# Lightning attention and a sin² feed-forward layer on one core: chunk 1's second projection by seven products of quarters, some forty copies free to run on another engine, and new order tables

## The chip, the core and the metric

One Trainium2 chip, one of its cores. The time is device microseconds from start to end of one execution. A core has a matmul engine (TensorE, PE in the profile, with its weight loads as PEld), VectorE (DVE), ScalarE (ACT), GpSimd (POOL) and SyncE (SP), each with its own list of instructions that it runs in order, and 16 DMA engines that move data between HBM and the on-chip memory. PE writes into eight accumulator banks of 128 x 512 f32 (PSUM).

## The reference, cut to what matters

```python
# attention: B, H, S, D = 4, 8, 768, 64; blocks along the sequence
intra = (q_blk @ k_blk.T * Dmask) @ v_blk          # Dmask[i, j] = lam**(i - j) for i >= j, else 0
inter = (q_blk * lam**(pos + 1)) @ kv_state
out   = intra + inter
kv_state = lam**block * kv_state + (k_blk * lam**(block - 1 - pos)).T @ v_blk
# feed-forward: x is out as [3072 tokens, 512], w_in [512, 2048], w_out [2048, 512]
h = x @ w_in
s = np.sin(alpha * h)
g = h + s * s / (alpha + 1e-09)
y = (g @ w_out).astype(np.float32)                 # the only output
```

## The kernel before

**Tiling.** The 3072 tokens are 24 blocks of 128 tokens for the attention and six chunks of 512 tokens (four blocks each) for the feed-forward layer. All matmuls take bf16 operands.

**Attention of a block.** q and k are scaled by powers of lam (`scale_block`, L454; the powers come from iotas on POOL and exponents on ACT at the start), transposed on PE (`piece_Q`, `piece_K`, `piece_T`; results copied to `qkT`), multiplied to scores in banks 1 and 2, which DVE multiplies by the mask into `Sm` (L623, "the mask product"), and multiplied with v (`part_O`, `piece_G`). Bank 7 holds the running state, which is copied to `Zc` or `Zd` (`part_Z`). The block's output is copied to `xT` (`part_O`'s `then`, `evict` L734). v is cast to bf16 on its way (`v2`). The first four blocks are made in smaller pieces ahead of everything else.

**First projection.** For each of 16 slices of 128 columns of w_in, `unit_A` (L807) runs four matmuls of 512 tokens into a bank; `unit_A2` (L845) does two slices for 256 tokens in eight matmuls. Here such a group of matmuls is called a unit. Behind each unit stand a sine on ACT (L832, L866), a square on ACT or POOL (L836/L837, L870/L871), and on DVE the sum h + s²/alpha into `gT` (L839, L874), which reads the unit's bank again and so sets it free. From chunk 1 on, the units share banks 4, 5 and 6.

**Second projection, two ways.** For chunks 0 and 1, `unit_B` (L880) runs 16 groups of four 512-wide matmuls (L887), and ACT copies each finished 128 x 512 result out (`osb`), from where ACT's queue stores it. For chunks 2 to 5 (`SC = 2`) the product of gT and w_out is split into quarters and made from seven products instead of eight: `weight_sums` (L914) forms five sums of quarters of w2 once (`Tw` in the ring `ws`, `Ta`, and two in place in `w2`; L930), `token_sums` (L933) forms for each quarter `p` of a chunk four sums of quarters of gT (two into `Xs`, two in place; L953) and, after product k = 1, four late ones in place (`late_sums`). `product` (L1037) runs one of the seven products for one half `u` of the rows: eight 256-wide matmuls (`unit_P`, L975), 14 such products in a chunk, in the order 3, 4, 2, 5, 1, 6, 7. `finish` (L1003) combines them: products 3 and 1 are copied (`kept`, on ACT), the others added or subtracted on DVE; SP stores the results. Each sum of quarters may run on POOL or DVE, as the tables say.

**Order.** Nothing is scheduled on the chip. `op` records every operation with what it reads and writes; `_Plan.ORDER` holds one list of operation numbers for each engine, written out by hand, and `_settle` goes through the lists; `emit` adds the semaphore waits, leaving out those that an earlier wait already covers. An operation whose engine is given as one name has to stand in that engine's list; one with several choices may stand in any of them. Pairs such as (42,112) in PE's list are fillers: so many matmuls of that many columns on unused data (`spin`, L1131), without a result.

**The main loop** (from L1136) runs the 16 units of chunk 0, the attention of blocks 4 to 11 between the groups of chunk 0's second projection and the units of chunk 1, and then for each chunk c from 2 to 5 its 16 units, the attention of the next blocks, the token sums of chunk c (for c >= SC) and the second projection of chunk c - 1. The weight sums stand ahead of the loops for chunks 2 and 3. After the loop come the 14 products of chunk 5. In chunk 2 (`c <= SC`) the attention's output takes bank 0 or 3, later one of banks 4 to 6 (`other()`).

**Other names that the change touches.** `QD` names which of the first four q scalings run on DVE. `cast_w1_first` (L381) casts the first half of w_in's first columns from `ws`, two 1024-column parts on DVE. The mask is made by POOL selects (`affine_select`), kept in a row by a common key `"select"`. `warm` is an exponent on ACT without use, ahead of the real ones.

## Time and profile before

Three runs took 210.68, 211.11 and 211.37 us, median 211.11. The profiled execution has a span of 209.8 us.

| | PE | DVE | ACT | POOL | DMA |
|---|---|---|---|---|---|
| busy, us | 203.5 | 160.3 | 158.7 | 126.9 | |
| share of the span | 97% | 76% | 76% | 60% | |
| instructions | 1975 | 266 | 294 | 130 | |
| 0 to 19 us | 16.00 | 12.61 | 13.02 | 10.59 | 99% |
| 193 to 209.8 us | 14.18 | 9.02 | 2.71 | 2.91 | 36% |

The granted clock of PE is 1.00 in all stages. The program moves 33.35 MB, of them 27.28 read from HBM. Of the chain that ended last, PE has 83%, DVE 6%, transfers 3% and SP's queue 3%; by line, the units of the first projection (L822, L856) hold 37%, the products (L975) 22%, the groups of the old second projection (L887) 13%.

How to read the rows that follow: a group's row has the line, the engine, the operation, the tiles written and read with their sizes, the count, then busy time in us, the mean of one in ns, and the engine's idle time just before them with what ended most of it. A row of the timeline or of the chain begins with the start in us and the duration. A row of windows has the stretch, its length and each engine's busy time with its number of instructions.

### The profile page before, as it was taken

The numbers are of one execution on the slowest core, as the hardware profiler recorded it, in microseconds if no ns is written. First come the engines' busy times: TensorE is split into PE (matmuls) and PEld (weight loads), VectorE is DVE, ScalarE is ACT, GpSimd is POOL, SyncE is SP. The second block draws the span as 40 slices with busy tenths as digits, with TensorE's granted clock in tenths as the row PEclk, the third lists the DMA queues.
The fourth block names the chain that finished last, engine by engine and source line by source line (L and its number), as shares of the span: only waits on it lengthen the run. The fifth ranks groups of instructions, "written<-read, shape, count | busy, mean of one in ns | idle before, by whom it ended". The sixth has DMA issues, their size and how long they took to land.

```text
span 209.8 us, 4867 instructions
## 1 busy us (share of the span) xinstructions
PE 203.5 (97%) x1975; PEld 134.3 (64%) x1975; DVE 160.3 (76%) x266; ACT 158.7 (76%) x294; POOL 126.9 (60%) x130
## 2 busy tenths in 40 slices
PE   7979999999999999999998999999999999999995
PEld 6847444457677776555555667766667765666894
DVE  4884557563999866868899799889698699777643
ACT  4949995968998989999997887787963889568210
POOL 7075354994469578679885392944581957378300
DMA  4999999999998999999999920190000004000514
GB/s 141 310 318 232 206 213 237 246 229 256 220 264 205 227 245 230 223 233 196 246 271 228 213 53 0 33 271 2 3 0 3 0 23 179 3 0 0 200 40 163
DMA packets 78998, 33.35 MB, mean 159 GB/s; under 512 B 55408, under 2 KB 76160, under 8 KB 78976
## 3 DMA queue, kind: packets, MB, share of 16 engines
q1 hardware_dynamic: 73744, 27.14, 56.2%
q0 software_dynamic: 3696, 3.67, 10.5%
q10 hardware_dynamic: 1536, 2.24, 3.3%
q8 instruction: 15, 0.25, 0.5%
q14 instruction: 7, 0.06, 0.1%
HBM read 27.28 MB, written 6.29 MB: 160 GB/s over the span
## 4 chain that ended last, share of the span: by engine, by line
PE 83%; DVE 6%; DMA 3%; SPq 3%; ACT 2%; issue 1%
PE bank L822 27%; PE bank L975 22%; PE bank L887 13%; PE bank L856 10%; DMA v<-in_v_dram 3%; PE bank L716 3%; SPq L315 3%; PE bank L612 3%; DVE gT L839 2%; PE bank L694 1%; DVE Sm L623 1%; PE bank L511 1%; PE bank L656 1%; DVE w L930 1%; PE bank L534 1%; PE bank L707 1%
## 5 line engine op out<-in xcount | busy, mean ns | idle before, releaser
L822 PE MATMUL bank<-xT,w 128*128 128x512 bf16 x296 | 70.5, 379 | 0.0
L839 DVE SCALAR_TENSOR_TENSOR gT<-u,rinv,bank 128x512 bf16<-128x512 bf16 x74 | 53.6, 742 | 18.2 <-ACT u L836 12.5
L832 ACT ACTIVATE t<-bank,alpha 128x512 bf16<-128x512 f32 x74 | 50.0, 684 | 21.0 <-PE bank L822 20.5
L822 PEld LDWEIGHTS bank<-xT,w 128*128 128x128 bf16 x296 | 28.3, 98 | 28.4 <-DVE gT L839 0.4
L836 ACT ACTIVATE u<-t 128x512 bf16<-128x512 bf16 x59 | 36.5, 628 | 1.3
L837 POOL TENSOR_TENSOR u<-t 128x512 bf16<-128x512 bf16 x15 | 16.0, 1066 | 34.1 <-ACT t L832 30.5
L953 POOL TENSOR_TENSOR gT<-gT 128x512 bf16<-128x512 bf16 x24 | 27.8, 1172 | 11.2 <-DVE Xs L953 6.0
L623 DVE TENSOR_TENSOR Sm<-bank,mask 128x1024 bf16<-128x1024 f32 x24 | 29.1, 1218 | 4.3 <-PE bank L648 1.8
L887 PE MATMUL bank<-w,gT 128*128 128x512 bf16 x128 | 31.4, 380 | 0.0
L874 DVE SCALAR_TENSOR_TENSOR gT<-u,rinv,bank 128x256 bf16<-128x256 bf16 x44 | 18.8, 476 | 7.8 <-ACT u L870 6.1
L472 POOL TENSOR_TENSOR qk<-q,Lq 128x512 bf16<-128x512 f32 x20 | 21.2, 1075 | 2.8 <-DMA q<-in_q_dram 2.8
L856 PE MATMUL bank<-xT,w 128*128 128x256 bf16 x176 | 22.2, 273 | 0.0
L492 POOL TENSOR_TENSOR qk<-k,Lk 128x512 bf16<-128x512 f32 x20 | 20.9, 1053 | 0.6 <-DMA k<-in_k_dram 0.6
L866 ACT ACTIVATE t<-bank,alpha 128x256 bf16<-128x256 f32 x44 | 18.9, 476 | 2.0 <-PE bank L856 1.5
L887 PEld LDWEIGHTS bank<-w,gT 128*128 128x128 bf16 x128 | 11.7, 98 | 12.2
L856 PEld LDWEIGHTS bank<-xT,w 128*128 128x128 bf16 x176 | 16.4, 98 | 3.5 <-issue 0.3
L953 POOL TENSOR_TENSOR Xs<-gT 128x512 bf16<-128x512 bf16 x13 | 16.1, 1235 | 1.5 <-DVE gT L839 1.4
L975 PE MATMUL bank<-w,gT 128*128 128x256 bf16 (+1 forms) x136 | 16.3, 266 | 0.0
L975 PE MATMUL bank<-w,Xs 128*128 128x256 bf16 (+1 forms) x136 | 16.0, 267 | 0.1
L975 PE MATMUL bank<-ws,gT 128*128 128x256 bf16 x128 | 15.8, 273 | 0.0
L975 PEld LDWEIGHTS bank<-w,gT 128*128 128x128 bf16 x136 | 12.6, 98 | 3.2
L975 PEld LDWEIGHTS bank<-w,Xs 128*128 128x128 bf16 x136 | 12.4, 98 | 2.8 <-DVE osb L1021 0.3
(101 smaller groups left out, 276.0 us busy)
## 6 DMA issues: line engine op xcount, KB each, us to landing
q<-in_q_dram SPq DMA_DIRECT2D x12, 512.0 KB, 6.2
k<-in_k_dram SPq DMA_DIRECT2D x24, 256.0 KB, 5.5
v<-in_v_dram SPq DMA_DIRECT2D x24, 256.0 KB, 5.4
out_dram<-osb SPq DMA_DIRECT2D x14, 256.0 KB, 2.5
w<-in_moe_w_out_dram POOLq DMA_DIRECT2D x4, 512.0 KB, 11.4
w<-in_moe_w_in_dram POOLq DMA_DIRECT2D x3, 512.0 KB, 9.0
ws<-in_moe_w_in_dram SPq DMA_DIRECT2D x2, 512.0 KB, 7.5
out_dram<-osb ACTq DMA_DIRECT2D x8, 128.0 KB, 4.0
```

The source lines that it names most:

```text
L472: lambda e, a=a: e.tensor_tensor(qk2[:, j:j + 2, 4 * a:4 * a + 4, :], q32[:, jq, 4 * a:4 * a + 4, :, :].rearrange("p h t d -> p t h d"), b ...
L492: lambda e: e.tensor_tensor(qk2[:, j, H:2 * H, :], block32(k32, jl), lk, ALU.mult), 1.05,
L623: op("DVE", lambda e: e.tensor_tensor(Sm[js][:, :, :], banks[:, 512 * b0:512 * b0 + 1024].rearrange("p (c i) -> p c i", i=128), bass.AP(ma ...
L822: ins = e.matmul(ps[hb][:, c0:c1], w1[:, kc, 128 * m:128 * (m + 1)], xT[x][:, kc, c0:c1], start=(kc == 0 and c0 == lo), stop=(kc == NKC - ...
L832: op("ACT", lambda e: e.activation(t16[ju][:, w], ps[hb][:, w], ACTF.Sin, scale=alpha[:, m:m + 1]), 0.69 if hi - lo == TCH else 0.475, [ba ...
L836: lambda e: (e.activation(u16[ju][:, w], t16[ju][:, w], ACTF.Square) if e is nc.scalar else e.tensor_tensor(u16[ju][:, w], t16[ju][:, w], ...
L839: op("DVE", lambda e: e.scalar_tensor_tensor(out=gT[g][:, m, w], in0=u16[ju][:, w], scalar=rinv[:, m:m + 1], in1=ps[hb][:, w], op0=ALU.mul ...
L856: ins = e.matmul(ps[hb][:, 256 * i:256 * i + 256], w1[:, kc, 128 * (m + i):128 * (m + i + 1)], xT[x][:, kc, lo:lo + 256], start=(kc == 0 a ...
L866: op("ACT", lambda e, i=i: e.activation(t16[ju][:, 256 * i:256 * i + 256], ps[hb][:, 256 * i:256 * i + 256], ACTF.Sin, scale=alpha[:, m + ...
L887: ins = e.matmul(ps[ob][:, w], gT[g][:, m, 128 * s4:128 * (s4 + 1)], w2[:, m, w], start=(m == 0), stop=(m == NM - 1),)
L953: e.tensor_tensor(dst, in0, in1, alu), 0, rd, wr))
L975: ins = e.matmul(ps[ob][:, lo + d0:lo + d1], lhs, rhs[:, d0:d1], start=first and p == 0, stop=(p == NM // 2 - 1), skip_group_check=True)
```

## The change

- `SC` goes from 2 to 1: chunk 1's second projection is made by the seven products too. Both sets of weight sums are recorded ahead of chunk 1's second half of units, chunk 1's token sums behind every second of these, and the second projection of chunk 1 by `product` (with chunk 2's attention outputs in one of banks 4 to 6).
- About forty copies and scalings that had a fixed engine, or one of two, may stand in the list of any of two or three: `AD` is ACT or DVE, `DP` DVE or POOL, `ADP` all three. They are the casts of w1, the first q scalings, the k scalings, the v casts, the copies of q and k transposes, of the state, of the attention outputs and of the second projection's results.
- POOL's selects lose their common key; instead `emit` makes a POOL operation that is marked `some`, and the one behind it, wait for the operation before it (`strict`). The exponents on ACT read `warm`, so that they stand behind it.
- All five order tables are new. The fillers, 102 in ten places of PE's list with 112 to 512 columns, become 22 of 512 columns at its head.

The core of the diff:

```diff
@@ class _Plan: ORDER @@
-            (42,112), 39, (30,128), 57, (11,128), 55, (1,128), 53, (1,128), 59, (8,128), 61, (1,512), 62,
-            (3,512), 65, 67, 69, 70, (3,512), 73, 75, 78, 80, 82, 85, (2,512), 87, 90, 91, 93, 124, 130, 140,
...
+            (22, 512), 39, 53, 59, 57, 55, 61, 62, 67, 69, 70, 65, 75, 78, 82, 73, 80, 87, 85, 90, 91, 93, 124,
+            130, 136, 140, 151, 147, 144, 159, 167, 163, 155, 175, 183, 171, 230, 228, 229, 191, 187, 206, 207,
...
@@ _ordered, emit @@
-        if d.eng != o.eng or d.dma is not None:
+        if d.eng != o.eng or d.dma is not None or d is o.strict:
...
+        last = None
+        for o in order:
+            if o.eng == "POOL" and o.dma is None:
+                if last is not None and (o.some or last.some):
+                    o.strict = last
+                    o.deps.add(last)
+                last = o
@@ sizes @@
-    SC = 2
-    QD = ((0, 0), (0, 2), (1, 0), (1, 2))
+    SC = 1
+    AD = (("ACT", 0, 0), ("DVE", 0, 0))
+    DP = (("DVE", 0, 0), ("POOL", 0, 0))
+    ADP = (("ACT", 0, 0), ("DVE", 0, 0), ("POOL", 0, 0))
@@ cast_w1_first @@
-                    op("DVE",
+                    op(AD,
@@ scale_block @@
-                            ported(op(QE(a, t),
+                            ported(op(DP,
...
-                        eng, dur = ("DVE", 0.68) if s + a < 3 else ("POOL", 1.05)
-                        ported(op(eng, lambda e, a=a: e.tensor_tensor(
+                        ported(op(DP, lambda e, a=a: e.tensor_tensor(
...
-                ported(op((("ACT", 0.62, 0.0), ("POOL", 1.05, 0.3)) if s > 11 else "ACT",
+                ported(op(ADP,
@@ part_Z, then @@
-                        op("ACT" if s < NP else (("ACT", 0.36, 0.0), ("DVE", 0.43, 0.0)), lambda e, r=r: (e.copy if e is nc.scalar else e.tensor_copy)(
+                        op(AD, lambda e, r=r: (e.copy if e is nc.scalar else e.tensor_copy)(
@@ unit_B @@
-                op("ACT", lambda e: e.copy(osb[jo][:, w], ps[ob][:, w]), 0.59, [bank(ob)], parts)
+                op(AD, lambda e: (e.copy if e is nc.scalar else e.tensor_copy)(osb[jo][:, w], ps[ob][:, w]), 0.59, [bank(ob)], parts)
@@ finish @@
-                    op("ACT", lambda e: e.copy(c1 if i == 1 else ny, got), 0.59 if n == 2 else 0.37, [bank(ob)], kc if i == 1 else kn)
+                    op(AD, lambda e: (e.copy if e is nc.scalar else e.tensor_copy)(c1 if i == 1 else ny, got), 0.59, [bank(ob)], kc if i == 1 else kn)
@@ main loop @@
             pieces = pieces_of(8, None, False) + pieces_of(10, 9, False)
+            if SC == 1:
+                weight_sums(True)
+                weight_sums(False)
             for i in range(8):
                 unit_A2(1, 2 * i, 1, (5, 6, 4)[(i + 2) % 3])
+                if SC == 1 and i % 2:
+                    token_sums(1, i // 2)
...
-                if c == SC + 1:
+                if c == SC + 1 and SC > 1:
                     weight_sums(False)
```

By the new tables, the first cast of w1 stands in ACT's list and the second in DVE's, chunk 1's sixteen token sums are ten on DVE and six on POOL, its four late ones two on each, chunk 5's four late sums are all on POOL, and the loads of w2 (issued from POOL's list) stand further behind in it.

More of the change, by code (lines that the diff above doesn't have):

```diff
@@ L31, in __init__ @@
         self.knows = None
+        self.some = False
+        self.strict = None
 class _Plan:
@@ L413, in _ @@
                 out=identf[:, :], in_=identf[:, :], pattern=[[-1, 128]], compare_op=ALU.not_equal,
[L414 removed]
+                fill=1.0, base=0, channel_multiplier=1), 0.5, ["identf"], ["identf"])
             op("DVE", lambda e: e.tensor_copy(ident[:, :], identf[:, :]), 0.2, ["identf"], ["ident"])
@@ L446, in _ @@
             op("ACT", lambda e: e.copy(alpha[:, :], ps[4][:, 0:NM]), 0.2, [bank(4), "warm"], ["alpha"])
-            def QE(s, a):
-                return "DVE" if (s, a) in QD else "POOL"
             def ported(o):
@@ L538, in piece_Q @@
                     if len(tbs) == 2:
-                        op("ACT", lambda e, a=a: e.copy(qkT[:, jt:jt + 2, 2 * a:2 * a + 2, :], tps[a]),
+                        op(AD, lambda e, a=a: (e.copy if e is nc.scalar else e.tensor_copy)(
+                            qkT[:, jt:jt + 2, 2 * a:2 * a + 2, :], tps[a]),
                            0.59, [bank(tbs[a])], [("qT", jt, a), ("qT", jt + 1, a)])
@@ L569, in piece_K @@
                 for t in range(2):
-                    op("ACT" if s else (("DVE", 0.43, 0.0), ("ACT", 0.6, 0.0)),
+                    op(AD,
                        lambda e, t=t: (e.copy if e is nc.scalar else e.tensor_copy)(qkT[:, jt + t, 4:8, :], tps[t]),
```

34 lines of the change are left out of this document (16 added, 18 removed), and 107 rows, old and new, of the table ORDER.

## The prediction, made before the changed kernel ran

> **What bounds the kernel now.** I read the page's first line, then the busy time by stage (cut where chunk 0 starts, where block 6 is scored, in chunk 2, where the loads end, where the last products begin), then the chain of waits.
>
> ```profile
> span 209.8 us, 4867 instructions
> ```
>
> ```profile
> 19.00:52.80 33.80, 33.80 (x243) 18.44 (x242) 19.42 (x30) 27.14 (x51) 19.58 (x17) 1.00 1.16 228
> 52.80:90.00 37.20, 37.20 (x432) 25.39 (x432) 31.27 (x58) 34.25 (x74) 26.56 (x27) 1.00 1.03 232
> 90.00:130.00 40.00, 39.33 (x345) 23.00 (x343) 35.45 (x52) 34.48 (x61) 28.41 (x25) 1.00 0.92 183
> 130.00:193.00 63.00, 63.00 (x517) 41.89 (x515) 52.56 (x83) 47.09 (x79) 38.83 (x35) 1.00 0.14 43
> ...
> sum 209.80, PE 203.51 PEld 134.30 DVE 160.35 ACT 158.69 POOL 126.87; mean PE 33.92 PEld 22.38 DVE 26.72 ACT 26.45 POOL 21.15
> ```
>
> The columns are the stretch, its length, then the busy time (and instructions) of PE, weight load, DVE, ACT and POOL, the granted clock and the DMA share. From 19 us to 193 the matmul engine has no hole but 0.67 us, in 90:130. So whatever leaves its list there is gained, unless another engine becomes the slower one. Next in line is the vector engine: 84% busy in 52.8:90 (31.27 of 37.20), 89% in 90:130.
>
> ```profile
> 7.63 6.83 DMA v<-in_v_dram
> ...
> 15.79 0.73 ACT xT L739
> ...
> 19.16 0.87 PE bank L856 x8
> ...
> 51.46 0.22 PE bank L511 x4
> ...
> 59.38 0.49 PE bank L534 x8
> ...
> 61.84 0.86 PE bank L887 x4
> ...
> 65.10 0.33 PE bank L612 x8
> 65.43 0.34 PE bank L707 x8
> 65.77 0.34 PE bank L716 x8
> 66.24 1.85 PE bank L856 x16
> ...
> 162.74 0.87 PE bank L975 x8
> ```
>
> The chain gives the start (a load of v that lands at 14.46, then ScalarE's copies in a row, then the first unit at 19.16) and the prices on the matmul engine: a group of the old second projection 0.86 (L887), a product of quarters 0.87 (L975), a unit of the first projection 0.87, one whole attention block 1.14 (65.10 to 66.24).
>
> **The change, part by part.**
>
> *Chunk 1's second projection.* 16 groups of four 512-wide matmuls go, 14 products of eight 256-wide ones come: 16 x 0.86 - 14 x 0.87 = 13.8 - 12.2, so **-1.6 us** on the engine that sets the end. No row leaves room for another size: both kinds ran back to back.
>
> *What it costs beside.* Chunk 1 now needs 16 token sums and four late ones, two copies and five additions for its results in place of four copies, and both sets of weight sums have to be ready two chunks' work earlier. The order tables put 12 of the 20 token sums on VectorE, 8 on GpSimd. The open engines also move work: by the tables v's casts go from ScalarE 20 and GpSimd 4 to ScalarE 5, GpSimd 10, VectorE 9; k's scalings on VectorE from 3 to 8; squares on GpSimd from 22 to 29. So ScalarE gets room that no part of the matmul engine waits for, and VectorE and GpSimd lose theirs. Prices:
>
> ```profile
> L839 DVE SCALAR_TENSOR_TENSOR gT<-u,rinv,bank 128x512 bf16<-128x512 bf16 x74 | 53.6, 742 | 18.2 <-ACT u L836 12.5 <-POOL u L837 5.2
> L623 DVE TENSOR_TENSOR Sm<-bank,mask 128x1024 bf16<-128x1024 f32 x24 | 29.1, 1218 | 4.3 <-PE bank L648 1.8 <-PE bank L612 1.5 <-PE bank L656 1.0
> L874 DVE SCALAR_TENSOR_TENSOR gT<-u,rinv,bank 128x256 bf16<-128x256 bf16 x44 | 18.8, 476 | 7.8 <-ACT u L870 6.1 <-POOL u L871 1.5
> L953 DVE TENSOR_TENSOR Xs<-gT 128x512 bf16<-128x512 bf16 x19 | 12.3, 658 | 0.1
> L953 DVE TENSOR_TENSOR gT<-gT 128x512 bf16<-128x512 bf16 x24 | 12.2, 532 | 0.1
> ...
> L726 DVE CAST xT<-bank 128x512 bf16<-128x512 f32 x7 | 5.1, 734 | 1.3 <-PE bank L716 1.1 <-PE bank L656 0.3
> ...
> L930 DVE TENSOR_TENSOR w<-w 128x1024 bf16<-128x1024 bf16 x3 | 3.3, 1105 | 0.0
> ...
> L930 DVE TENSOR_TENSOR ws<-w 128x1024 bf16<-128x1024 bf16 x2 | 1.4, 700 | 0.0
> L516 DVE COPY qkT<-bank 128x512 bf16<-128x512 bf16 x5 | 2.1, 424 | 2.3 <-PE bank L511 2.3
> ...
> L571 ACT COPY qkT<-bank 128x512 bf16<-128x512 bf16 x3 | 1.7, 588 | 1.6 <-PE bank L560 1.5
> L543 ACT COPY qkT<-bank 128x1024 bf16<-128x1024 bf16 x1 | 1.0, 1012 | 0.8 <-PE bank L534 0.8
> ...
> L953 POOL TENSOR_TENSOR gT<-gT 128x512 bf16<-128x512 bf16 x24 | 27.8, 1172 | 11.2 <-DVE Xs L953 6.0 <-DVE gT L953 5.0
> ```
>
> These are groups with their shapes kept apart: count, busy time, mean of one in ns, idle time before them. I counted the new tables where it is tightest, from the scores of block 6 to the first half of product 5 of chunk 1. VectorE's list there, from block 6's mask product to the token sum that this product reads, holds 73 instructions: 38 gT of 256 columns x 0.43 = 16.2; 2 gT of 512 x 0.72 = 1.4; 7 mask products x 1.21 = 8.5; 10 token sums x 0.57 (24.5 for 43) = 5.7; 3 weight sums in place x 1.10 and one other x 0.70 = 4.0; 12 copies and additions at 0.4 to 0.73 = 6.1. That is 41.9. Neighbours overlap in such sums (all of VectorE's groups add up to 170, its busy time to 160.35), so x 0.94: **39.5 us**. The matmul engine's list between the same two points: 31 units, groups and products x 0.865 = 26.9; seven attention blocks x 1.14 = 8.0; two pairs of q transposes x 0.49 and four of k x 0.22 = 1.9: **36.8 us**. VectorE works in order, a unit's bank isn't free before its gT is made, and there are three such banks; so the matmul engine can't run away, and if VectorE never idled the matmul engine would still lose 2.7 us. Both ends of this term: 0 if all sums run at their shortest (0.42 for a token sum, 0.70 for a weight sum: 2.7 less, all of it); 7.6 if VectorE does no better than the 89% of 90:130 (39.5 / 0.89 = 44.4, less 36.8). I take **+4.0**, near full use, since that engine has run without a hole when it was behind. The **0.67** of 90:130 goes, as later stretches are under this lateness and the weight sums are no longer in them.
>
> How a sum gets long is seen here:
>
> ```profile
> 107.05 1.16 POOL L953 TENSOR_TENSOR gT<-gT 128x512 bf16<-128x512 bf16 x1
> ...
> 107.22 1.27 DVE L953 TENSOR_TENSOR Xs<-gT 128x512 bf16<-128x512 bf16 x1
> 181.09 0.42 DVE L953 TENSOR_TENSOR gT<-gT 128x512 bf16<-128x512 bf16 x1
> ```
>
> The sum on VectorE that began at 107.22 inside one of GpSimd's (107.05 to 108.21) ended at 108.49 and took 1.27 in place of 0.42. [...]
>
> *The start.* The landing of v at 14.46 stays. Behind it ScalarE's new list has, ahead of the last two xT pieces, six Zd copies, a kT copy, a v cast, a cast of w1 (1024 columns; it was VectorE's) and xT of block 0. Against before, the kT copy (0.59) and the w1 cast come, two xT copies of 0.73 leave for VectorE. The cast of w1 on ScalarE is in no row; the nearest is ScalarE's 1024-wide copy, 1.01, and the shortest it could be is a 512-wide one, 0.59; I take 1.0. So 0.59 + 1.0 - 1.46 = 0.1, and the first unit, which has xT of block 0 behind that cast now, loses what it was ahead, about 0.9 at most: **+0.5** (from -0.5, if the shorter list counts more, to +1.5, if VectorE's mask products, which now stand behind a v cast of its own that waits for its load, end last). GpSimd's mask selects stand ahead of its iotas and wait for each other, so the exponents and the q scalings come some tenths later; behind them the 22 fillers that replace 102 end about 1 us after the first q transposes were made. v's landing covers both; without it they would cost that 1 us.
>
> The timeline's row for the k transposes that end at 12.20:
>
> ```profile
> 11.38 0.82 PE L560 MATMUL bank<-ident,qk 128*128 128x128 bf16 x8
> ```
>
> And the windows of the fillers alone (length, PE, weight load, clock, DMA share):
>
> ```profile
> 1.60:4.20 2.60, 2.60 (x29) 2.60 (x30) 1.00 0.53 136
> 5.30:6.80 1.50, 1.50 (x30) 1.50 (x28) 1.00 1.12 353
> ```
>
> These windows show the fillers alone: 29 of 112 columns in 2.60 us, then 30 of 128 in 1.50, so 0.80 against 0.39 ns a column: the matmul engine begins at half its rate. Without later fillers it could fall back. The longest hole in the new list is from the last k transposes (12.20 before) to v's landing, 2.3 us. I put 0 into the sum. [...]
>
> *The loads of w2.* Three of the four now stand behind five squares and more on GpSimd's list, so two are issued some 12 us later.
>
> ```profile
> w<-in_moe_w_out_dram POOLq DMA_DIRECT2D x4, 512.0 KB, 11.4
> ```
>
> The first of them is issued at about 29 (nine units of 0.87 from 19.7 and two engines' work behind) and its groups come at about 37; 11.4 later would be 40. But that landing time was queueing behind the other loads (DMA share 1.16), and those are fewer by then. 0, with 3 at the far end.
>
> *The end.* The same 14 products follow. But all four late sums of chunk 5 now stand on GpSimd, behind five other instructions: nine x 1.17 = 10.5 us, for a product that comes about as late. **+0.3** (0 to 1).
>
> *Queues.* SP gets chunk 1's four stores ahead of a load of v and transposes that aren't due for some 10 us; ScalarE loses its four. Nothing waits: 0.
>
> Sum against the profiled execution: 209.8 - 1.6 - 0.7 + 4.0 + 0.5 + 0.3 = 212.3. The median of the runs, 211.1, is 1.3 above that execution, so **213.6 us**.
>
> **Rivals.**
>
> 1. *VectorE keeps up* (the other side): the sums run at their shortest because the new tables keep them off GpSimd's. 209.8 - 1.6 - 0.7 + 0.5 + 1.3 = 209.3, faster. For it: 16% of VectorE was idle in 52.8:90. Against: ten token sums and three weight sums in place are 9.0 us of it (5.7 + 3.3). It decides as soon as VectorE's list is under 36.8 us.
> 2. *VectorE only reaches 89%* since it waits for squares on GpSimd, whose in-order list is mixed with scalings that wait for loads (DMA share 1.03 in 52.8:90): 7.6 in place of 4.0, 217.2. For it: gT's idle time, 12.5 and 5.2, was just such waits.
> 3. [...] By its totals GpSimd goes from 127 to about 149 us, some 84% of the time after the start. A sum that begins anywhere in one of 1.17 waits 0.58; at 84% 0.49, against 0.15 in the mean now: 14 sums x 0.34 = 4.8 more, 218.4. Against: the tables place sums with care today (0.15).
> 4. *The matmul engine falls back to half rate* before the first unit and needs at least the 2.6 us of the start again, half of it lost: +1.3, 214.9. For it: the holes that the fillers filled. Against: none reaches the 2.6 us.
> 5. *About no change*: VectorE loses just 1.5 to 2: 211.1.
>
> **How the numbers follow.** 0.3% (0.6 us) is about what a measurement of this kernel tells from no change. Forecast 0.37, rivals in their order 0.25, 0.14, 0.07, 0.10, 0.07. Faster by more than 0.3%: rival 1, 0.25; within: rival 5, 0.07; slower: the others, 0.68. The range goes from rival 1 to just over rival 2, **209.2 to 217.8**, and leaves out rival 3 and the ends; the forecast's own range is 212 to 215.5.
>
> **What would show it.** Right: L975 with 112 more matmuls and L887 with 64 fewer; in the stretch from the scores of block 6 to chunk 1's products the matmul engine several us short of full and VectorE above 95%, the chain running through gT and the sums; the first unit at about 19.7. Wrong: a matmul engine without holes there (rival 1); holes whose releaser is GpSimd's square or a load (rival 2); token sums of 0.9 on VectorE (rival 3); units of 1.7 us around 20 (rival 4).

## The result, and the profile after

The changed kernel takes 231.09 us (median of four runs, 230.48 to 232.37) beside 211.17 for the kernel before on the same chip: ratio 1.0955, 95% interval 1.0914 to 1.0996. It is slower, as forecast, but by 19.9 us where 2.5 had been said, and outside the range. Its profiled execution has a span of 228.7 us, 18.9 more than before's. Of the experiments below, r3, r4 and r6 have the time of a single run and r9 and r11 the median of three, since one run of each was disturbed.

The head of its page, and the chain of waits by engine:

```profile
span 228.7 us, 4821 instructions
PE 202.9 (89%) x1921; PEld 134.2 (59%) x1943; DVE 193.0 (84%) x293; ACT 147.8 (65%) x267; POOL 155.9 (68%) x153
PE 42%; DVE 33%; ACT 10%; POOL 8%; issue 3%; DMA 1%; ACTq 1%; DVEq 0%; POOLq 0%
```

PE has as much to do as before (202.9 against 203.5 us) and now idles for 25.8 us instead of 6.3. DVE is busy for 33 us more with 27 more instructions; of the chain that ended last it holds a third, where it held 6%.

To see where, both executions are cut at the same points of DVE's work: its 1st, 50th, 70th, 86th, 102nd and 118th addition into `gT` (roughly the start; chunks 0 and 1; and chunks 2, 3, 4, 5). Windows of the kernel before, first and last stage left out, with the columns of the prediction's table:

```profile
22.10:82.20 60.10, 60.10 (x578) 37.32 (x576) 42.45 (x74) 51.15 (x102) 40.40 (x38) 1.00 1.07 230
82.20:109.10 26.90, 26.90 (x229) 14.23 (x228) 23.08 (x36) 25.35 (x48) 21.86 (x21) 1.00 1.20 237
109.10:140.70 31.60, 30.93 (x283) 20.52 (x281) 28.17 (x44) 25.28 (x43) 18.81 (x17) 1.00 0.60 132
140.70:170.80 30.10, 30.10 (x275) 20.45 (x274) 25.03 (x39) 21.50 (x37) 17.84 (x16) 1.00 0.03 11
170.80:196.20 25.40, 25.40 (x177) 16.99 (x176) 21.13 (x33) 18.12 (x30) 16.22 (x14) 1.00 0.14 53
```

The same stages of the kernel after:

```profile
24.60:84.80 60.20, 55.33 (x564) 35.73 (x566) 52.31 (x87) 43.31 (x86) 47.75 (x45) 1.00 1.01 210
84.80:120.70 35.90, 30.94 (x275) 20.23 (x281) 33.75 (x46) 25.73 (x48) 28.02 (x25) 0.95 0.79 161
120.70:153.30 32.60, 29.52 (x269) 19.33 (x271) 31.88 (x47) 22.42 (x37) 20.01 (x19) 1.00 0.62 137
153.30:186.00 32.70, 30.46 (x270) 20.08 (x273) 27.53 (x43) 20.43 (x33) 20.67 (x18) 1.00 0.19 53
186.00:214.10 28.10, 25.90 (x177) 17.07 (x176) 22.97 (x33) 17.74 (x28) 20.09 (x18) 1.00 0.10 38
```

| stage | start | chunks 0, 1 | 2 | 3 | 4 | 5 | end |
|---|---|---|---|---|---|---|---|
| length before | 22.1 | 60.1 | 26.9 | 31.6 | 30.1 | 25.4 | 13.6 |
| length after | 24.6 | 60.2 | 35.9 | 32.6 | 32.7 | 28.1 | 14.6 |
| PE idle before | 3.0 | 0 | 0 | 0.7 | 0 | 0 | 2.6 |
| PE idle after | 5.6 | 4.9 | 5.0 | 3.1 | 2.2 | 2.2 | 2.8 |

The table's last rows are length less PE's busy time. The chunk-2 stage also holds most of chunk 1's products (in the kernel before its groups), and loses 9.0 us: 5.0 of holes and 4.0 in which PE is busy longer. Most of the 4.0 is work moved there from the stage ahead, where PE has 4.8 less to do but is no sooner done; about 1.7 of it is PE at half its clock (further down). Chunks 4 and 5, which the prediction had left alone, lose 5.3 between them. In the chunk-2 stage DVE is busy for 33.75 of 35.90 us (94%), in chunk 3's for 31.88 of 32.60 (98%).

Now the groups with their shapes kept apart:

```profile
L961 DVE TENSOR_TENSOR gT<-gT 128x512 bf16<-128x512 bf16 x29 | 25.4, 885 | 0.3 <-POOL Xs L961 0.2
L961 DVE TENSOR_TENSOR Xs<-gT 128x512 bf16<-128x512 bf16 x20 | 14.0, 704 | 0.1
L502 DVE CAST v<-v 128x512 bf16<-128x512 f32 x8 | 6.8, 856 | 0.0
L499 DVE TENSOR_TENSOR qk<-k,Lk 128x512 bf16<-128x512 f32 x5 | 5.3, 1063 | 0.0
L435 DVE CAST mask<-maskf 128x128 bf16<-128x128 f32 x3 | 4.4, 1472 | 0.0
L961 POOL TENSOR_TENSOR gT<-gT 128x512 bf16<-128x512 bf16 x31 | 38.7, 1259 | 4.9 <-DVE Xs L961 1.6 <-PE bank L983 1.1 <-DVE gT L847 1.1
```

DVE's token sums went from 532 and 658 ns to 885 and 704. By the shortest one, 0.42 us, 49 sums would be 20.6 us; they took 39.4, so 18.8 beyond the shortest. Before it was 43 sums, 24.5 us, 6.4 beyond. Instructions that read a bank kept their lengths (L847: 741 ns, before 742; the mask product 1218 both times). What has grown, then, are DVE's token sums, its scalings of k (689 before, 1063 and 960 now) and one of its three mask casts (3.98 us for 0.22), none of which reads a bank, and GpSimd's sums in place (1172 to 1259; those into `Xs` went from 1235 to 1196).

PE's largest wait in the table of waits:

```profile
PE bank L830 <- DVE gT L847: 9.3, 10, 2.5
```

Ten units waited 9.3 us in all for DVE to free their bank; the longest single one is 2.5 us.

### The profile page after: what moved, and what is told of

Same layout as the page of the kernel before. It is cut to its first block, busy times and chain, and to the rows that moved or that the text cites. A ratio compares the mean times of both kernels' runs of the same rounds, so it can differ in the third digit from the quotient of the medians.

```text
span 228.7 us, 4821 instructions
## 1 busy us (share of the span) xinstructions
PE 202.9 (89%) x1921; PEld 134.2 (59%) x1943; DVE 193.0 (84%) x293; ACT 147.8 (65%) x267; POOL 155.9 (68%) x153
## 4 chain that ended last, share of the span: by engine, by line
PE 42%; DVE 33%; ACT 10%; POOL 8%; issue 3%; DMA 1%; ACTq 1%; DVEq 0%; POOLq 0%
PE bank L830 15%; PE bank L983 14%; DVE gT L847 8%; DVE gT L961 6%; DVE gT L882 4%; DVE Sm L631 4%; PE bank L864 4%; PE bank L895 3%; ACT t L840 3%; POOL u L845 2%; ACT u L844 2%; DVE Xs L961 2%; POOL Xs L961 1%; DVE v L502 1%; PE bank L620 1%
## 5 line engine op out<-in xcount | busy, mean ns | idle before, releaser
L840 ACT ACTIVATE t<-bank,alpha 128x512 bf16<-128x512 f32 x74 | 50.5, 684 | 35.0 <-PE bank L830 34.4
L847 DVE SCALAR_TENSOR_TENSOR gT<-u,rinv,bank 128x512 bf16<-128x512 bf16 x74 | 53.4, 741 | 14.3 <-ACT u L844 8.4
L845 POOL TENSOR_TENSOR u<-t 128x512 bf16<-128x512 bf16 x24 | 26.0, 1090 | 35.1 <-ACT t L840 35.0
L961 POOL TENSOR_TENSOR gT<-gT 128x512 bf16<-128x512 bf16 x31 | 38.7, 1259 | 4.9 <-DVE Xs L961 1.6
L844 ACT ACTIVATE u<-t 128x512 bf16<-128x512 bf16 x50 | 31.4, 629 | 2.9 <-DVE gT L847 1.6
L631 DVE TENSOR_TENSOR Sm<-bank,mask 128x1024 bf16<-128x1024 f32 x24 | 29.0, 1218 | 2.4 <-PE bank L656 1.6
L961 POOL TENSOR_TENSOR Xs<-gT 128x512 bf16<-128x512 bf16 x20 | 23.9, 1196 | 6.9 <-DVE gT L847 4.7
L961 DVE TENSOR_TENSOR gT<-gT 128x512 bf16<-128x512 bf16 x29 | 25.4, 885 | 0.3 <-POOL Xs L961 0.2
L882 DVE SCALAR_TENSOR_TENSOR gT<-u,rinv,bank 128x256 bf16<-128x256 bf16 x44 | 18.9, 473 | 4.4 <-POOL u L879 3.8
L983 PE MATMUL bank<-w,gT 128*128 128x256 bf16 (+1 forms) x168 | 21.2, 275 | 0.3 <-DVE kept L1000 0.2
L983 PE MATMUL bank<-ws,gT 128*128 128x256 bf16 x160 | 20.1, 273 | 0.1
L983 PE MATMUL bank<-w,Xs 128*128 128x256 bf16 (+1 forms) x168 | 20.0, 268 | 0.0
L983 PEld LDWEIGHTS bank<-w,gT 128*128 128x128 bf16 x168 | 15.9, 100 | 5.6 <-issue 0.6
L983 PEld LDWEIGHTS bank<-w,Xs 128*128 128x128 bf16 x168 | 15.6, 98 | 3.5
L983 PEld LDWEIGHTS bank<-ws,gT 128*128 128x128 bf16 x160 | 15.4, 98 | 3.6 <-DVE gT L847 0.6
```

The lines of the kernel that those rows point to most:

```text
L631: op("DVE", lambda e: e.tensor_tensor(Sm[js][:, :, :], banks[:, 512 * b0:512 * b0 + 1024].rearrange("p (c i) -> p c i", i=128), bass.AP(ma ...
L840: op("ACT", lambda e: e.activation(t16[ju][:, w], ps[hb][:, w], ACTF.Sin, scale=alpha[:, m:m + 1]), 0.69 if hi - lo == TCH else 0.475, [ba ...
L844: lambda e: (e.activation(u16[ju][:, w], t16[ju][:, w], ACTF.Square) if e is nc.scalar else e.tensor_tensor(u16[ju][:, w], t16[ju][:, w], ...
L845: e.tensor_tensor(u16[ju][:, w], t16[ju][:, w], t16[ju][:, w], ALU.mult)), 0,
L847: op("DVE", lambda e: e.scalar_tensor_tensor(out=gT[g][:, m, w], in0=u16[ju][:, w], scalar=rinv[:, m:m + 1], in1=ps[hb][:, w], op0=ALU.mul ...
L882: op("DVE", lambda e, i=i: e.scalar_tensor_tensor(out=gT[g][:, m + i, lo:lo + 256], in0=u16[ju][:, 256 * i:256 * i + 256], scalar=rinv[:, ...
```

## The experiments

In the trace of the kernel after, the 16 of DVE's 49 token sums that began outside all compute instructions of GpSimd took 0.40 to 0.42 us. Of the 33 that began inside one, 31 took over 0.5, up to 1.40, and each of these ended 0.28 us behind the end of that instruction. GpSimd's own token sums took 1.15 us at their shortest and up to 1.60 where they began inside an instruction of DVE that uses no bank. The additions into `gT`, which read a bank, show none of this: the 44 of 512 columns that began inside one of GpSimd's instructions took 0.73 to 0.75 us, the other 30 took 0.72 to 0.75. These waits between GpSimd's instructions and those of DVE that go from SBUF to SBUF (tiles that are no bank) are called the exclusion here.

Theory X: the exclusion, which the new tables didn't reckon with, makes DVE late, in all stages. Its rivals: squares on GpSimd that DVE waits for (theory O below); chunk 1's own work, which is too much for DVE (theory W); one bad place (the mask cast); the start.

**A single instruction: the mask cast.** The timeline of the kernel after, where PE stands for 2.55 us, from 34.75 to 37.30 (the expectation below has 2.7 at 34.4):

```profile
32.61 3.98 DVE L435 CAST mask<-maskf 128x128 bf16<-128x128 f32 x1
32.62 0.81 POOL L325 DMA_DIRECT2D w<-in_moe_w_out_dram  x1
33.45 2.06 POOL L480 TENSOR_TENSOR qk<-q,Lq 128x512 bf16<-128x512 f32 x2
35.45 1.04 POOL L499 TENSOR_TENSOR qk<-k,Lk 128x512 bf16<-128x512 f32 x1
36.51 0.74 DVE L847 SCALAR_TENSOR_TENSOR gT<-u,rinv,bank 128x512 bf16<-128x512 bf16 x1
```

A cast of 128 columns (0.22 us elsewhere) lasts until the last of GpSimd's three scalings ends at 36.49. It didn't end either while GpSimd only issued a DMA, up to 33.43. The run moves this cast, and the mask piece on GpSimd that it needs, to the start:

```diff
 "POOL"
-            21, 22, 24, 18, 12, 14, 25, 13, 15, 29, 41, 43,
+            21, 22, 24, 18, 12, 14, 25, 13, 15, 27, 29, 41, 43,
...
-            149, 27, 169, 106,
+            149, 169, 106,
 "DVE"
-            20, 17, 16, 33, 26, 19, 42, 44, 45, 23, 60, 46,
+            20, 17, 16, 33, 26, 19, 42, 44, 45, 23, 60, 28, 46,
...
-            170, 158, 28, 178,
+            170, 158, 178,
```

> The changed kernel with one thing put back: the third mask's select (GpSimd) and cast (VectorE) stand at the start of their lists again. In the changed kernel this cast of 128 columns took 3.98 us on VectorE (32.61 to 36.51) while GpSimd ran a DMA issue and three scalings, and the matmul engine stood for 2.7 us at 34.4. If that one wait is a loss of its own: 231.1 - 2.7 = 228.4, and the rest of the profile as it was. If the sums meet GpSimd's instructions by chance anyway, what follows stays as late as it is (227.5 to 229). If the later collisions come only from this early lateness, the gain is far more than 2.7: under 222.

230.4 us (ratio 1.088, 1.066 to 1.110): 0.7 less than the kernel after, which this interval can't tell from nothing, and 2 us above what was expected of a loss of its own. In the profiled execution the cast now takes 0.2 to 0.5 and the stage of chunks 0 and 1 is 57.4 instead of 60.2, so 2.8 us are won there. They are lost ahead of it. Windows of this run:

```profile
11.00:14.00 3.00, 1.12 (x22) 0.78 (x23) 2.84 (x6) 2.19 (x5) 1.44 (x2) 0.88 1.18 300
14.00:17.00 3.00, 2.99 (x48) 2.18 (x46) 3.00 (x3) 1.10 (x3) 3.00 (x5) 0.50 1.02 267
```

PE, busy for 1.12 of 3 us, falls to half its clock at about 13.3 and stays there for 10 us; the first `gT` comes at 27.8 instead of 24.6.

**DVE's token sums without reads.** DVE's sums of quarters of gT are left out: each is a fill of the same tile, which reads nothing.

```diff
@@ token_sums @@
+                              e.memset(dst, 0.5) if e is nc.vector else
                               e.tensor_tensor(
```

> The changed kernel with VectorE's 49 token sums replaced by memsets of the same tiles (the sums are left out, the output is wrong there), which read nothing from SBUF; GpSimd's lists and all waits stay. A memset of 128x512 took 0.485 us at the start, a token sum 0.81 in the mean here and 0.41 at its shortest. Theory X (VectorE's SBUF-to-SBUF instructions and GpSimd's exclude each other): VectorE's busy time falls by 49 x 0.32 = 16 us or more, GpSimd's sums fall from 1.23 towards 1.05, and the time by 10 to 16: 215 to 221. Theory O (the order of the lists, GpSimd's squares behind scalings and DMA issues, sets the pace): VectorE only gets more idle time, 227 or more.

219.09 us (ratio 1.0345, 1.0112 to 1.0578; the interval lies apart from that of the kernel after, but is wide), 12 us less than the kernel after, and 10.2 less by the spans of the two profiled executions (218.5 and 228.7). The groups of this run:

```profile
L961 DVE MEMSET gT<- 128x512 bf16 x29 | 14.1, 485 | 2.3 <-DVE Xs L961 0.5 <-POOL Xs L962 0.3 <-issue 0.2
L961 DVE MEMSET Xs<- 128x512 bf16 x20 | 9.7, 485 | 1.3 <-DVE gT L847 0.3
```

The number of instructions on DVE is unchanged, and a fill is even longer than the shortest sum (0.485 against 0.42). But both groups have the same mean, 0.485, which is also the length of the fill at the start: GpSimd didn't hold them up. They are 15.6 us shorter than the sums, and 10 to 12 of that is time. GpSimd's sums, which theory X had falling towards 1.05 us, took 1.22 in place and 1.18 into `Xs`, instead of 1.26 and 1.20. Cut at the same additions into `gT` as above, chunks 2 to 5 of this run:

```profile
85.80:116.60 30.80, 29.03 (x277) 19.58 (x281) 29.12 (x46) 25.11 (x47) 27.95 (x26) 1.00 0.91 200
116.60:147.10 30.50, 29.52 (x271) 19.64 (x273) 28.67 (x47) 22.99 (x38) 19.34 (x19) 1.00 0.76 150
147.10:178.80 31.70, 30.43 (x270) 20.17 (x273) 26.05 (x43) 20.44 (x33) 19.96 (x18) 1.00 0.20 55
178.80:204.20 25.40, 25.30 (x176) 17.13 (x176) 18.45 (x32) 17.74 (x28) 18.77 (x18) 1.00 0.11 42
```

Against the kernel after they are 5.1, 2.1, 1.0 and 2.7 us shorter, so the late stages lose by the sums too. (Each of the two executions has one stretch of 3.4 us at half clock, the kernel after in chunk 2's stage, this one in that of chunks 0 and 1.) Up to 84.8 us, where the kernel after is 2.6 behind before, nothing is gained (85.8, or some 84.1 without the half clock): most of that isn't lost by these sums.

**The squares.** All 29 squares on GpSimd go to ScalarE in the tables, at the same places of the order; DVE's casts of v and scalings stay. (In this kernel and in all others but r1, r2 and r3 the weight sums that write into `ws` wait for both casts of w1, whichever engine makes them.) The second run of the pair has the fills of the run before as well, with the same part left out.

```diff
@@ "ACT" @@
-            81, 95, 94, 126, 125, 132, 131, 137, 141, 152, 148, 153, ...
+            81, 95, 94, 126, 125, 127, 132, 131, 133, 137, 138, 141, 142, 152, 148, 149, 153, ...
@@ weight_sums @@
-                                  0, keys, wr))
+                                  0, keys, wr, after=[last["cast", x] for x in (0, 256)] if i < 4 else ()))
```

> The changed kernel with all 29 squares of GpSimd (1.09 us each, 31.6 us) put on ScalarE (0.63 each, 18 us) right behind their sines. GpSimd's busy share of the span falls from 68% to about 56%. Theory X: a sum meets GpSimd less often, by 31.6/155.9 = 20%, so VectorE's 32 us over the shortest times fall by some 6, and the waits for GpSimd's squares go: 220 to 226. Theory O, the squares as what is late: 218 to 222. If VectorE's own work is the bound: 229 or more.

> The second run's memsets in place of VectorE's token sums (sums left out) and the fourth run's squares on ScalarE together. Alone they gave 219 and 231. If collisions are the whole of it, the squares add nothing: 217 to 220. If GpSimd's list is the second bound, seen only once VectorE is free: 212 to 216.

229.11 us for the squares alone, in a single run, and 220.3 (ratio 1.044, 1.031 to 1.057) with the fills, beside 231.09 and 219.09: 2.0 less and 1.2 more. Theory X had expected 220 to 226 for the first, so that was a miss. GpSimd's busy time falls from 155.9 to 124.0, but DVE's sums stay long:

```profile
L964 DVE TENSOR_TENSOR gT<-gT 128x512 bf16<-128x512 bf16 x29 | 21.3, 744 | 0.1
```

So it isn't late squares that DVE waits for, or for 2 us at most. What sums run into is mostly GpSimd's other work: in the timeline of the kernel after, 31 of DVE's 49 token sums take over 0.5 us, 21 of them beside GpSimd's own token sums, 6 beside its scalings and 4 beside its squares.

**Chunk 1 by groups in the new order.** `SC` goes back to 2; the groups stand where the products stood, chunk 1's sums go.

```diff
-    SC = 1
+    SC = 2
...
@@ main loop, attention outputs of chunk 2 @@
-                                3 - 3 * (done // 4 % 2) if c <= SC else other())
+                                other())
```

> The changed kernel's engines and order, but chunk 1's second projection by 16 groups of four again (SC = 2, groups in the places of the products, copies and stores on ScalarE, the four in-place weight sums behind chunk 1's last group): 20 token sums fewer. Theory W (the work of chunk 1's sums and results is what is too much): 214 or less. Theory X or O (the collisions or the order of all other work): 20 x 0.8 x 12/20 = 10 us less on VectorE, of which half shows: 221 to 227.

229.62 us. Inconclusive on chunk 1's stage: the copies of the groups' results came too early in ScalarE's list, which waited 3.0 us there for a store and 3.0 more for groups. But chunks 4, 5 and the end take 32.7, 28.1 and 14.6, to the tenth as in the kernel after, though chunk 1's sums are gone. These stages lose without chunk 1's sums.

**Which part of the order loses.** Three runs join parts of the two orders: the kernel after with before's order from chunk 3 on (r6); with before's order up to 18 us (r7); and the kernel before, chunk 1 by groups, with the new order from chunk 3 on (r8). The head of GpSimd's list in r8, which is before's, against that of the kernel after:

```diff
 "POOL"
-            21, 22, 24, 18, 12, 14, 25, 13, 15, 29, 41, 43, 49, 52, 30, 102, ...
+            12, 13, 14, 18, 15, 21, 22, 24, 25, 27, 29, 30, 50, 47, 48, 102, ...
```

> The changed kernel up to the end of chunk 2, then the engines and the order of before for all that the kernel before began from chunk 3's units on (407 operations, the weight sums left in place). From chunk 3 on the changed kernel lost 1.0, 2.6, 2.7 and 1.0 us a stage against before, 7.3 in all, with the same work on the matmul engine. If these orders and engines are what loses it: 223 to 225. If the loss only follows from being late or out of step after chunk 2: 229 to 232.

> The changed kernel with the engines and the order of before for the 183 operations that the kernel before began ahead of its first unit (fillers too), then the changed lists. Its first gT ended at 24.6 us, before's at 22.1. If the start is a loss of its own: 231.1 - 2.5 = 228.6. If being late at the start puts the sums out of step with GpSimd: 222 or less. If the matmul engine's clock falls without those fillers, that goes too: another 1 to 2 less.

> The kernel before (chunk 1 by groups, its own engines and order) up to chunk 2's end, then the changed engines and order for the 421 operations that the changed kernel began from chunk 3 on. If the new order itself loses the 7.3 us there: 211.1 + 7.3 = 218.4. If it only loses when it is late: 211 to 212.5.

They took 241.18, 230.79 (ratio 1.0936, 1.0891 to 1.0982) and 225.26 us (1.0674, 1.0610 to 1.0739). r6 has a hole of 16.5 us where the two orders meet, and r7's first units waited 2.9 us for a load of w_in, so neither total says much; r8, expected at 218.4, has stages of 31.7 and 33.7 us for chunks 2 and 3, around its joint. The stages behind say more. Windows of r8 over chunks 4 and 5:

```profile
147.60:180.30 32.70, 30.45 (x270) 20.07 (x273) 27.53 (x43) 20.43 (x33) 20.66 (x18) 1.00 0.13 41
180.30:208.40 28.10, 25.90 (x177) 17.08 (x176) 22.97 (x33) 17.74 (x28) 20.09 (x18) 1.00 0.10 38
```

And of r6:

```profile
169.30:200.00 30.70, 30.00 (x271) 20.37 (x274) 24.93 (x40) 22.28 (x38) 17.81 (x16) 1.00 0.09 25
200.00:225.30 25.30, 25.14 (x173) 16.95 (x175) 21.08 (x33) 18.08 (x30) 16.21 (x14) 1.00 0.14 52
```

With the new order the two stages take 32.70 and 28.10 even behind chunks 0 and 1 made as before (r8); with the old one 30.70 and 25.30 even when everything comes 29 us late (r6). The work in them is the same by the diff, apart from the engine on which it stands. So the new late order, with its choice of engines, costs about 5 us in these two stages ((32.7 - 30.7) + (28.1 - 25.3) = 4.8); r2 got back 3.7 of the same 5.3 in the kernel after.

**Tables that reckon with the exclusion.** Six kernels have the changed code (or the same with `SC = 2`) and tables laid out once more, with free choice of the open engines, from the shortest duration that each kind of instruction had in the traces. One set counts DVE's and GpSimd's SBUF instructions as excluding each other, the other doesn't; nothing else differs in how they were made. In the first three the first 18.5 us are as before, in the others the first 48. Where GpSimd's list in r12 (with) first leaves that of r13 (without):

```diff
 "POOL"
             107, 149, 169, 157, 108, 199, 195, 196, 197,
-            326, 329, 211, 212, 213, 219, 330, 262, 352, 281,
+            326, 329, 211, 212, 213, 219, 214, 220, 262, 260,
```

> The changed kernel's code (chunk 1 by products, open engines), with the start of before, and the five order tables made anew behind 18.5 us: positions and engines moved until the lists, with each instruction's shortest duration from the traces, end earliest, where a VectorE instruction that goes from SBUF to SBUF and a GpSimd instruction wait for each other. No work is left out. Theory X (what the changed tables lack is this exclusion, not room on the engines): the 1.6 us of chunk 1 and the 0.7 of the hole come out, 207.5 to 210.5. Theory W (chunk 1's sums are too much for VectorE whatever the order): 214 or more.

> The same code, start and way of making the tables as in the run before, with the one difference that the two engines are taken not to wait for each other. Theory X: VectorE's token sums then meet GpSimd's by chance, as in the changed kernel (0.81 us in the mean), and the time is 224 to 232. If the changed tables are slow for another reason: within 2 us of the run before.

> Chunk 1 by groups again (SC = 2), open engines, tables made with the exclusion as in the first of these runs. If the 16 groups against 14 products are worth their 1.6 us once the collisions are gone, this one is 1 to 2 us above the first of these runs; if VectorE's load eats it, the same within 0.6.

> As the run with tables made with the exclusion (225.4), but all that the kernel before began in its first 48 us stands in the old engines and order, loads included; what was made anew lies behind. In that run the matmul engine stood 6.8 us at 27 and some 4 us more by 47, behind loads of q that landed 14 us after their issue beside the loads of w_in and w_out, and from 50 us on it ran dense. Theory X: with these loads back the whole is dense, 211.1 - 1.6 - 0.7 and up to 1 of new holes: 208 to 210.5. If VectorE can't carry chunk 1's sums in any order (theory W): 213 or more.

> The same as the run before it, first 48 us included, made in the same way but with the two engines taken not to wait for each other. Theory X: 222 to 232, all of it lost behind 48 us, with VectorE's token sums near 0.8 us in the mean. Another cause: within 2 us of the run before it.

> Chunk 1 by 16 groups (SC = 2), first 48 us as before, the rest made anew with the exclusion and open engines. If the products are worth their 1.6 us: 1 to 2 above the first of these three. If their sums cost VectorE what they save: the same within 0.6.

| kernel | us | ratio (95%) |
|---|---|---|
| r9 products, with | 224.58 | 1.0649 (1.0587 to 1.0711) |
| r10 products, without | 237.25 | 1.1219 (1.1168 to 1.1271) |
| r11 groups, with | 228.96 | 1.0853 (1.0822 to 1.0885) |
| r12 products, with | 220.52 | 1.0430 (1.0371 to 1.0489) |
| r13 products, without | 232.80 | 1.1019 (1.0958 to 1.1079) |
| r14 groups, with | 217.37 | 1.0302 (1.0242 to 1.0362) |

Both pairs differ by some 12 us (237.25 - 224.58 = 12.7; 232.80 - 220.52 = 12.3), about what the fills gave. But r9 and r12 are 14 and 10 us above the most that theory X allowed, in the range of theory W, and r10 and r13 are 5 and 1 above what it gave for them; only the last two runs part the two theories. And groups against products come out 4.4 us slower in r11 and 3.1 faster in r14, so sets of tables made in one way scatter by several us, and of the 12 only the sign and the rough size are safe. The sums into gT on DVE, in r12 and then in r13:

```profile
L965 DVE TENSOR_TENSOR gT<-gT 128x512 bf16<-128x512 bf16 x42 | 18.9, 465 | 0.1
```

```profile
L965 DVE TENSOR_TENSOR gT<-gT 128x512 bf16<-128x512 bf16 x42 | 27.5, 671 | 1.1 <-POOL Xs L965 1.0
```

Same count, 206 ns apart each. Reckoning with the exclusion also makes such tables use GpSimd less (113.8 us busy in r12, 129.4 in r13). What r12 still loses is seen in its waits of PE:

```profile
PE bank L868 <- ACT osb L913: 2.9, 1, 2.9
PE bank L987 <- ACT v L506: 2.0, 1, 2.0
PE bank L624 <- POOL v L506: 1.5, 1, 1.5
```

The first and the third are a copy and a cast that stand behind a late load of v in an in-order list (ScalarE waits 3.25 us for one, GpSimd 2.38 for another); the second, a cast of v, stands behind other work of ScalarE. r9 and r11 lost more in the first way: scalings on DVE in r9, and a cast of v on GpSimd in r11 (11.4 us), stood ahead of their loads' landing. DVE's waits in r9, from 20 to 50 us:

```profile
DVE qk L484 <- DMA q<-in_q_dram: 6.4, 1, 6.4
DVE qk L503 <- DMA k<-in_k_dram: 3.0, 1, 3.0
```

**With the loads as slow as they are.** The last two have before's order for the first 40 us and reckon with the exclusion and with the landing times that r12's trace showed. r16 has chunk 1 by groups (`SC = 2`). GpSimd's list of r15 against r12's:

```diff
 "POOL"
             107, 149, 169, 157, 108, 199, 195, 196, 197,
-            326, 329, 211, 212, 213, 219, 214, 220, 262, 260,
+            326, 260, 332, 261, 280, 285, 263, 262, 335, 376,
```

> Chunk 1 by products, open engines, tables made with the exclusion, the first 40 us as before, and now with loads and stores as slow as r12's trace shows them (5 to 7 us for a load of 256 or 512 KB, issues a microsecond or more apart, 3 to 6 us for a store in the first 120 us). r12 still lost 3 us by 57, 1 at 62, 5 between 97 and 115 and 1.5 at 135, each behind such a transfer (a copy of results that waits for its buffer's store, casts of v that wait for the load). Theory X: those go, 208 to 212. Theory W: 215 or more, with VectorE full and no transfer in the matmul engine's waits.

> The same with chunk 1 by 16 groups (SC = 2). If the products are worth their 1.6 us, 1 to 2 above the run before; if not, the same within 0.6 or below it.

r15 takes 212.78 us (ratio 1.0078, 1.0057 to 1.0098), r16 210.68 (0.9984, 0.9967 to 1.0001). r15 lies between the most that theory X allowed, 212, and the least of theory W, 215. Groups of r15, and its engines' busy time:

```profile
PE 200.8 (95%) x1999; PEld 138.5 (66%) x2023; DVE 172.6 (82%) x313; ACT 158.7 (75%) x292; POOL 99.6 (47%) x108
```

```profile
L965 DVE TENSOR_TENSOR gT<-gT 128x512 bf16<-128x512 bf16 x44 | 19.0, 456 | 0.2 <-POOL Xs L965 0.2
L965 DVE TENSOR_TENSOR Xs<-gT 128x512 bf16<-128x512 bf16 x27 | 10.7, 417 | 0.0
```

71 sums on DVE now take 29.7 us, where 49 took 39.4; with 20 more instructions DVE is busy for 20 us less than in the kernel after. The same seven products for chunk 1 and the same open engines, with before's first 40 us and another order and choice of engines behind, are 18.3 us faster. Chunk 1's work therefore isn't what costs 20 us. How much of the 18.3 is due to the exclusion, how much to the start, the loads and a GpSimd that is busy for 99.6 us instead of 155.9, no run parts.

It doesn't pay, either. r15 is 2.1 us slower than r16 (the intervals of the two ratios lie apart). The products' records in r15 add up to 13.8 us more than in r16 and the groups' to 15.3 less, so PE seems to have about 1.5 us less to do, though its busy time is just 0.2 shorter (some records of the groups are missing in both traces); but it idles for 10.5 us (span 211.3 less 200.8) instead of 7.7 (208.7 less 201.0), and of these 2.8 us, 1.8 lie in the stage with chunk 1's products (2.2 against 0.4), where it waits for `gT` (0.6), a transposing load (0.6), the copy of a product (0.5) and a sum (0.2). No kernel tried beats the one before by more than its measurement can tell.

## Why the prediction was wrong: point by point

**Direction and place: right in part.** In the stretch where DVE's list was counted as too long, DVE is busy for 41.0 of 43.1 us (95%), PE waits for `gT`, and the chain runs through DVE. But of the 19.5 us of holes that are new (25.8 less 6.3), only some 4.5 lie in it.

**-1.6 for fewer groups: not seen in time.** r15 against r16 has about -1.5 by the records of PE's products and groups, but the total went the other way by 2.1.

**-0.7 for the old hole: wrong.** Chunk 3's stage has 3.1 us of holes instead of 0.7.

**+4.0 for DVE's list: the step that failed.** It priced ten token sums at 0.57, the mean of the kernel before, times 0.94 for overlap, and put nothing for the other 39. That mean isn't a property of the instruction: in the kernel before, the 29 sums that began outside GpSimd's compute instructions took 0.41 to 0.43 and the 14 others up to 1.37, and the new tables change every place. Measured, the sums' means are 0.70 and 0.89. By chance alone, as an estimate, a sum that meets GpSimd busy for 68% of the span (155.9 of 228.7) and waits half of one of its sums (1.26) loses 0.43; the trace has 18.8 / 49 = 0.38. Before, chance would have given 0.60 x 0.59 = 0.35, and the trace has 0.15: the old order kept the two apart, the new one doesn't. In its own stretch the term came to 7.1: the 73 instructions on DVE took 43.1 us (55.17 to 98.29) where 39.5 had been counted, the ten sums among them 7.9 where 5.7 had, and PE took 43.9 (54.73 to 98.66) for its 36.8, about 1.7 of that at half clock. The larger error is the nothing for the rest: r2's fills give back 5.1 us in chunk 2's stage, whose first 13.9 us alone lie in that stretch, and 6.1 in the stages behind it.

**+0.5 for the start: mis-sized.** The first `gT` comes 2.5 later (24.6 against 22.1). The first unit began at 20.11 instead of 19.16, about the 0.9 named there. The rest is in the squares behind it: the first two stand on GpSimd now, end at 24.13, and DVE has waited 3.8 us for the first `gT`; before, ScalarE made the first square in 0.63. No row of the prediction had that. r7 was to settle the start and didn't.

**+0.3 for the end, and nothing for the stages between: wrong.** The end takes 1.0 more, chunks 3 to 5 take 6.3 more. "Later stretches are under this lateness" was an assumption without a row: in r8 chunk 1's products aren't ahead of them, and chunks 4 and 5 lose the same.

**The loads of w2: 0 held in itself,** though the mask cast that ended behind one of them made a hole of 2.55 us on PE; that instruction was in no term.

**The clock: 0 was wrong.** Rival 4 had it fall at the start; it fell later. Windows of the kernel after:

```profile
88.00:91.00 3.00, 1.05 (x8) 0.81 (x10) 3.00 (x6) 1.94 (x5) 3.00 (x3) 1.00 0.64 132
91.00:92.00 1.00, 0.90 (x3) 0.34 (x3) 1.00 (x3) 0.00 (x0) 1.00 (x3) 0.57 0.00 0
92.00:94.00 2.00, 2.00 (x10) 1.23 (x9) 1.99 (x5) 1.32 (x2) 1.64 (x2) 0.50 0.99 76
```

After 1.95 us of holes in 3 us, PE runs at half rate for 3.4 us, which costs about 1.7. In these holes PE waits for `gT`, so it is a price of DVE's lateness, not a cause of its own. That a hole has to reach 2.6 us, which rival 4 was held against, no run shows.

**The rivals.** Rival 3, sums that wait longer for a busier GpSimd, was the right mechanism, with 4.8 us as its price: 0.34 more for each of 14 sums. The size for one sum was fair (0.23 more than before on all sums, by 0.38 less 0.15), though its 84% for GpSimd was too high: from the first `gT` on GpSimd is busy for 142.3 of 204.1 us, 70%; the row named for it, token sums of 0.9 on DVE, came (0.885). The count was 14 of 49, and casts, scalings and GpSimd's own side weren't in it. It was put at 0.07 and left outside the range because "the tables place sums with care today"; that holds for the old tables only. Rival 1's sums at their shortest are nearly there in r15 (456 and 417 ns), and even that kernel isn't faster than before. Rival 2 falls by r4 and r5, and by DVE's 94% and 98% in the stages of chunks 2 and 3; rival 5 by the time.

What is shown, and what isn't: that sums on DVE without reads give 10 to 12 us back, all of it from chunk 2's stage on; that tables that reckon with the exclusion and those that don't differ by some 12, twice; that the same code can run in 212.8. The remaining 6 us or so between 219.1 (r2) and 212.8 (r15) weren't separated; candidates are the start (r2's first `gT` is 3.2 us later than before's), the mask cast, and the casts and scalings that r2 leaves as they are. That the exclusion also lengthens the casts and the scalings is seen in the trace of the kernel after (a cast of v took 0.42 us outside GpSimd's instructions and up to 1.39 inside one, a scaling of k by `Lk` 0.68 and up to 1.64), but no run took it out for them alone.

## What to carry to other kernels

The mean duration of an instruction in a trace holds its neighbours (a token sum on DVE took 0.42 us alone, 0.57 in the mean before and 0.80 after): before pricing a new order by it, take the shortest of its kind and work out anew what it will meet. For DVE's sums beside a busy GpSimd, GpSimd's busy share times half of one of its instructions is a first estimate for each of them, all through the kernel (0.43 for a measured 0.38 here); an order that keeps the two apart pays less (0.15 before), and orders made without it lost some 12 us here. A "no further cost" for later stages needs its own row as much as a cost does.

## What the runs showed of the hardware that was not expected

Some instructions on DVE were held through several GpSimd instructions in a row, though all 31 token sums over 0.5 us in the kernel after ended 0.28 us behind the one that they began in. Besides the mask cast (3.98 us for 0.22; 3.97 in r2, r3 and r6, at the same place), the timeline of r9 has it for a cast of v, 0.42 when undisturbed:

```profile
43.03 1.51 POOL L503 TENSOR_TENSOR qk<-k,Lk 128x512 bf16<-128x512 f32 x1
43.57 3.34 DVE L506 CAST v<-v 128x512 bf16<-128x512 f32 x1
44.51 2.12 POOL L942 TENSOR_TENSOR ws<-w 128x1024 bf16<-128x1024 bf16 x1
```

It began inside the first (43.03 to 44.54) and ended only after the second (46.63). It isn't casts alone: a weight sum on DVE took 3.43 us in r13, through three of GpSimd's scalings, and one 3.76 in r11, beside a scaling and a weight sum there. Of the token sums of all traces a single one (1.42 us, in r11) waited through two of GpSimd's instructions. What decides it stays open. Not lengthened were the fills of r2 (0.485 us in the mean of both groups) and `gT`'s additions (741 ns, before 742).

The clock fell after 1.95 us of holes within 3 us, and at the start of r1 for 10 us, but not after the single hole of 2.55 us at 34.75 in the kernel after. In r2 the same hole, 2.54 us long, came 0.6 us later, and there the clock fell to half behind it, from 38.7 to 42.1. So the length of a hole alone doesn't decide it. The stretches at half clock last 3.41 us in these two kernels and in r7, 6.83 in r8, 10.24 at the start of r1 and 17.07 in r6: one, two, three and five times 3.41. What else decides whether the clock falls, no run tested.
